# Causal masks of a fused attention and ELU-MLP kernel: products on VectorE against affine selects on GpSimd, in a newly planned order

## The chip, the cores and the metric

The kernel runs on one core of a Trainium2 chip. The metric is the device time of one execution in microseconds (us), given as the median of several runs; a profiled execution has a time of its own and a trace. The engines are TensorE (PE, with its weight loads as PEld), VectorE (DVE), ScalarE (ACT), GpSimd (POOL) and SyncE (SP). POOL and SP also issue most of the DMAs. Each engine works through its own instructions strictly in order.

## The reference, cut to what matters

The inputs are q, k and v with 8 batches, 8 heads, 576 positions and 64 columns per head, and 16 "beacon" keys and values per batch and head. The beacons stand ahead of the keys and are seen by every query; among the 576 keys, a query sees only those up to its own position. The result of the attention is laid out as 4608 tokens of 512 columns and goes through two matrix products with an ELU between them.

```python
scores = scale * np.matmul(q, k_all.transpose(0, 1, 3, 2))
causal[:, Nb:] = np.triu(np.ones((S, S), dtype=bool), k=1)
scores = np.where(causal, -1000000000.0, scores)
a = np.exp(scores - scores.max(-1, keepdims=True))
a /= a.sum(-1, keepdims=True) + 1e-09
x = np.matmul(a, v_all)          # then to (4608, 512)
h = x @ w_in
g = np.where(h > 0.0, h, np.exp(np.minimum(h, 0.0)) - 1.0)
out = g @ w_out
```

## The kernel before, in words

**The order.** All work is cut into some thirty kinds of steps, and the string at the end of the kernel (run, L793) lists 1430 of them in one hand-over order. A step is a word such as `x.3.4` or `m.3.0.1`; its fields are the batch or tile and the part of it. The list does not synchronize the engines with each other: it fixes the order in which each engine gets its own instructions, and waits between engines come from the data alone. So what a step's place decides is what stands ahead of it on its own engine.

**Attention.** A batch b has 13 chunks of scores (batch 0 has 16 smaller ones). `S.b.i` (L318) multiplies keys by queries on PE into PSUM, keys along the partitions; pairs of heads p = 0 to 3 follow each other along the columns, and parts that the mask would remove whole are not computed at all. `x.b.i` (L333) is the exponential on ACT, from PSUM into the tile et in SBUF, in 16-bit floats. What is left of the mask is a triangle of 128 columns in each block of keys; it is applied to et after the exponential by `m`.

**The masks.** For batches 1 to 7 there are four steps per batch, `m.b.d.g` (from L344): d is a half of the heads (two pairs, four heads), g = 0 takes the key blocks 0 and 1 in one product, of 128 partitions by 1024 elements, with the constant triangle triu; g = 1 takes blocks 2 and 3 in one such product and block 4 (80 partitions by 320 elements) in another. All are `tensor_tensor` products on DVE in L338. Batch 0 has 12 steps `m.0.p.g` by pairs, with one to three smaller products each.

**After the masks.** `D.b.d.n` (L396, DVE) adds key blocks into one tile ahead of the row sums; `L.b.d` (L376, L422, PE) forms the row sums and a first part of the output; `n.b.d` (L437, L440, ACT) inverts them; `W.b.d` (L376, PE) multiplies by v; `M.b.d.i` (L474, DVE) scales the result into xT, the MLP's input.

**The MLP.** Tile t has 512 tokens (tiles 0 and 1 have 256 each). `F.t.i` (L514, PE) is a piece of the first product, `e.t.i` (L524, ACT) its exponential. The other side of the ELU is either `u.t.i` (a rectifier, on ACT in L530, or with `.v` on DVE in L532) with `k.t.i` (L544, DVE), or `r.t.i` (L551, DVE) with `g.t.i` (L556, DVE). `Z.t.n` (L566, DVE) forms sums and differences of quarters for a Strassen-like second product, `Q.t.a.b` (L618, PE) is a run of its matmuls, and `J.t.n` drains PSUM (L628 on ACT, or with `.v` on DVE; L635 on DVE) and sends the result out by SP. For the last two tiles the first product is of this kind too (`P`, `K`, `E`, `U`, `V`, `X`, `H`).

**GpSimd.** It issues the loads: q and k of batches 0 to 2 (`lq`, L136), v (`lv`, L144 and L149), the weights (`wi`, L160; `wo`, L163), and for batches 3 to 7 copies of q and k within DRAM (`lk`, L769), which SP's transposing DMAs (`lt`, L776) bring into SBUF. It also makes the identity and triu (`ident`, `tri`; L236, L238) and fills the beacon keys and padding of batches 3 to 7 (`lp`, L785, L786). The drains of the transposed q and k of batches 0 to 2 are `ck` on ACT and `cq` on DVE (both L277). The eight DMA semaphores of POOL are used in turn, so its DMA waits for the landing of the eighth before it; what is behind that DMA on POOL waits too.

Of the kernel before, what the change touches and what calls it, by code (L numbers as in the profile page):

```python
# [17 lines left out]
def kernel(  # L18
# [787 lines left out]
    x.0.3.1 lv.0.2 m.0.1.0 m.0.2.0 m.0.0.0 L.0.A m.0.1.2 n.0.A m.0.0.2 T.1.0.0 wi.2 m.0.3.2
    cq.1.0.0 S.0.2.1 W.0.A.1 x.0.2.1 W.0.A.0 S.0.1.1 x.0.1.1 T.1.1.0 M.0.A.1 S.0.2.2 M.0.A.0
    x.0.2.2 F.0.5 cq.1.1.0 e.0.5 lv.0.3.4 m.0.2.2 wi.1 m.0.0.3 m.0.1.3 S.1.5 S.1.1 x.1.5 m.0.3.3
    F.0.4 x.1.1 lq.1.0.4.8 wi.0 m.0.2.3 L.0.B cb.1.1 e.0.4 W.0.B.1 n.0.B S.1.3 cb.1.3 u.0.4.v
    M.0.B.1 u.0.5.v F.0.2 x.1.3 e.0.2 r.0.2 S.1.4 x.1.4 S.1.0 x.1.0 F.0.3 T.1.3.0 ck.1.3.0  # L810
    W.0.B.0 g.0.2 wi.3 k.0.4 S.1.12 m.1.0.0 k.0.5 M.0.B.0 e.0.3 F.0.1 x.1.12 T.1.2.0 S.1.10
    r.0.3 g.0.3 F.1.0 cq.1.2.0 cb.1.2 e.0.1 u.0.1 x.1.10 k.0.1 F.1.1 e.1.0 S.1.8 lq.2.0.0.4
    u.1.1.v u.1.0 k.1.0 x.1.8 F.0.0 e.1.1 S.1.9 S.1.6 u.0.0.v lq.2.0.4.8 F.0.6 k.1.1 x.1.9
    lp.3.1 e.0.0 T.2.1.0 F.1.3 x.1.6 u.0.6.v e.0.6 cq.2.1.0 S.1.11 cb.2.0 lv.1.0.1 e.1.3 x.1.11
    S.1.7 k.0.0 F.0.7 S.1.2 u.1.3.v F.1.5 x.1.7 x.1.2 T.2.0.0 k.0.6 lv.1.2.3.4 u.0.7.v e.0.7
    m.1.1.1 T.2.2.0 ck.2.0.0 u.1.5.v ck.2.2.0 m.1.1.0 wo.1 e.1.5 m.1.0.1 F.1.6 wo.3 k.0.7 L.1.1
    L.1.0 wo.0 F.1.2 e.1.6 wo.2 k.1.5 lk.3.0 u.1.6.v lk.3.1 F.1.4 cb.2.1 cb.2.2 n.1.1 M.1.1.0
    W.1.0 k.1.6 n.1.0 M.1.0.0 u.1.2 W.1.1 lv.2.2.3.4 u.1.4 M.1.0.1 lk.4.0 e.1.2 lv.3.2.3.4 k.1.3
    S.2.4 e.1.4 x.2.4 F.1.7 M.1.1.1 k.1.4 u.1.7 e.1.7 F.2.13 T.2.3.0 S.2.8 u.2.13 k.1.7 F.2.12
    e.2.13 x.2.8 F.2.9 u.2.12 cq.2.3.0 S.2.3 e.2.12 k.2.13 S.2.1 e.2.9 wt.1.0 k.1.2 x.2.3 F.2.2  # L820
    e.2.2 lv.2.0.1 Z.1.3.B Q.1.0.7 x.2.1 Q.1.7.14 u.2.9.v S.2.2 S.2.0 u.2.2 k.2.12 F.2.6 k.2.9
    Q.1.14.21 x.2.0 x.2.2 F.2.15 cb.2.3 wt.1.1 e.2.6 wt.2.1 u.2.6 u.2.15 Q.1.21.28 e.2.15
    m.2.0.0 S.2.6 S.2.5 wt.2.0 F.2.4 J.1.0 x.2.5 F.2.10 Z.1.1.B Z.1.2.B S.2.11 x.2.6 Q.1.28.35
    lt.3.0 lp.3.0 lt.3.1 k.2.15 e.2.4 wt.3.1 u.2.4.v k.2.4 Q.1.35.42 x.2.11 S.2.7 x.2.7 k.2.2
    S.2.9 J.1.1 e.2.10 F.2.7 Q.1.42.49 u.2.7.v lk.4.1 Z.1.4.B u.2.10 Q.1.56.63 F.2.11 D.2.0.0
    x.2.9 S.2.10 S.2.12 wt.3.0 e.2.7 k.2.10 F.2.1 x.2.12 Q.1.49.56 J.1.2 Q.1.63.70 u.2.11 e.2.11
    wt.4.1 k.2.7 Q.1.70.77 k.2.6 F.2.3 S.3.0 m.2.0.1 x.2.10 u.2.1 e.2.1 D.2.0.1 J.1.3.v S.3.2
    D.2.0.2 D.2.0.3 x.3.0 F.2.14 e.2.3 x.3.2 Q.1.77.84 k.2.1 Q.1.84.91 r.2.3 k.2.11 L.2.0 n.2.0
    e.2.14 J.1.4 lk.5.1 W.2.0 wt.4.0 Q.1.91.98 M.2.0.0 M.2.0.1 H.1.2 S.3.4 u.2.14 F.2.5 m.2.1.0
    x.3.4 e.2.5 S.3.8 u.2.5 m.2.1.1 x.3.8 S.3.10 Q.1.98.105 lk.5.0 F.2.0 k.2.5 x.3.10 e.2.0  # L830
    lv.3.0.1 k.2.14 L.2.1 g.2.3 J.1.5 n.2.1 u.2.0.v W.2.1 F.2.8 M.2.1.0 M.2.1.1 u.2.8 F.3.6
    S.3.3 e.2.8 x.3.3 H.1.1 S.3.6 F.3.13 e.3.6 k.2.8 lt.4.0 x.3.6 lk.6.0 lp.4.1 Q.1.105.112
    k.2.0 Q.2.0.7 S.3.1 u.3.13.v Z.2.3.B S.3.12 Q.2.7.14 lp.4.0 u.3.6 F.3.4 e.3.13 J.1.6.v
    x.3.12 Q.2.14.21 lt.4.1 x.3.1 Z.2.1.B S.3.11 u.3.4 x.3.11 S.3.9 x.3.9 F.3.2 k.3.6 J.2.0.v
    Q.2.21.28 Z.2.2.B e.3.2 e.3.4 S.3.7 k.3.13 S.3.5 x.3.5 m.3.0.0 r.3.2 Q.2.28.35 F.3.8 g.3.2
    F.3.12 x.3.7 S.4.1 lt.5.0 S.4.0 Q.2.35.42 e.3.8 J.2.1 u.3.8 e.3.12 Q.2.42.49 m.3.0.1 r.3.12
    g.3.12 F.3.15 x.4.1 D.3.0.0 D.3.0.1 D.3.0.2 D.3.0.3 x.4.0 S.4.2 S.4.5 Q.2.49.56 J.2.2 x.4.2
    k.3.4 x.4.5 F.3.10 S.4.4 Z.2.4.B lt.5.1 e.3.15 x.4.4 S.4.3 u.3.10.v lp.5.1 m.3.1.0 x.4.3
    r.3.15 Q.2.56.63 Q.2.63.70 L.3.0 g.3.15 lk.6.1 e.3.10 k.3.10 n.3.0 W.3.0 lp.5.0 M.3.0.0
    M.3.0.1 F.3.7 u.3.7 e.3.7 F.3.3 S.4.7 S.4.11 F.3.9 lv.4 J.2.3.v u.3.3 x.4.11 k.3.7 D.3.1.0  # L840
    m.3.1.1 D.3.1.1 D.3.1.2 e.3.3 e.3.9 u.3.9 Q.2.70.77 k.3.3 k.3.8 Q.2.77.84 F.3.11 D.3.1.3
# [103 lines left out]
```

## Time and profile before

| what | value |
|---|---|
| median of 3 runs | 330.53 us (330.32 to 330.69) |
| the profiled execution, its own time | 329.86 us |
| its span, first to last instruction | 328.2 us |
| around the span | 1.66 us |
| granted TensorE clock | 1.0 in all of it |
| GpSimd: share of the span, instructions | 26%, 109 |

Busy time of an engine is the union of its instructions' spans. Matmuls overlap each other and their ends are modelled, so a PE that is busy throughout may still not be at its peak; the distance from one matmul's start to the next tells more. Idle time of an engine is put down to what ended it.

### The profile page before, as it was taken

To read this page: it belongs to the slowest core of one execution; us is meant where nothing else is said; L and a number is where in the kernel's file an instruction comes from. 1 tells how busy PE (TensorE), PEld (TensorE's weight loads), DVE (VectorE), ACT (ScalarE), POOL (GpSimd) and SP (SyncE) were. 2 spreads that over 40 slices of the span, in tenths; PEclk is the share of its full clock that TensorE was granted. 3 is DMA by queue.
4 is the path that set the end of the run, shared out by engine and by line. 5 is a ranking of instruction groups with operands and counts; after the bars stand their busy time and mean duration, and the time that the engine had idled before them with its cause. 6 is when DMAs were issued, how large, how long until landed. Compare 5 with 4: busy or idle time off the path is not lost.

```text
span 328.2 us, 8827 instructions
## 1 busy us (share of the span) xinstructions
PE 318.5 (97%) x3648; PEld 215.7 (66%) x3648; DVE 296.9 (90%) x527; ACT 276.4 (84%) x449; POOL 85.2 (26%) x109
## 2 busy tenths in 40 slices
PE   7879999999999999999999999999999999999995
PEld 4656766566555655566555665566665888888884
DVE  2677998999998999999989989999999999999992
ACT  2979999998889897999999888988699598889930
POOL 8973791742705626004010500000000000000000
PEclk9999999999999999999999999999999999999999
DMA  9999999999999999995922792010110021111113
GB/s 115 169 190 206 172 167 185 151 151 154 174 173 154 136 172 151 188 116 61 160 82 58 77 106 84 12 34 2 66 34 33 2 96 34 34 65 34 35 64 128
DMA packets 130520, 34.65 MB, mean 106 GB/s; under 512 B 112816, under 2 KB 130480, under 8 KB 130480
## 3 DMA queue, kind: packets, MB, share of 16 engines
q0 software_dynamic: 95840, 18.49, 69.1%
q1 hardware_dynamic: 33920, 15.34, 23.8%
q8 instruction: 28, 0.46, 0.6%
q10 hardware_dynamic: 720, 0.26, 0.3%
q14 instruction: 12, 0.10, 0.1%
HBM read 37.22 MB, written 15.34 MB: 160 GB/s over the span
## 4 chain that ended last, share of the span: by engine, by line
PE 72%; DMA 12%; ACT 7%; POOL 4%; DVE 3%; issue 2%; DVEq 0%; POOLq 0%
PE ops L618 27%; PE hps L514 22%; DMA v<-in_v_dram 10%; PE hps L706 8%; PE sc L318 5%; ACT et L333 5%; PE ut L376 5%; PE sx L618 2%; POOL scr L769 1%; POOL v L149 1%; DMA kst<-in_k_dram 1%; ACT e L524 1%; POOL w_out L163 1%; DVE qkp L396 1%; PE lt L422 1%
## 5 line engine op out<-in xcount | busy, mean ns | idle before, releaser
L333 ACT ACTIVATE et<-sc 128x1024 f16<-128x1024 f32 (+2 forms) x114 | 104.2, 968 | 8.1 <-PE sc L318 7.6
L514 PE MATMUL hps<-xT,w_in 128*128 128x512 f16 (+1 forms) x512 | 110.7, 353 | 0.3 <-DVE gt L556 0.3
L618 PEld LDWEIGHTS <-gt 128*128 128x128 f16 x864 | 83.0, 98 | 21.1 <-issue 2.9
L524 ACT ACTIVATE e<-hps 128x512 f32<-128x512 f32 x112 | 66.7, 615 | 9.0 <-PE hps L514 4.1
L514 PEld LDWEIGHTS <-w_in 128*128 128x128 f16 x512 | 46.8, 98 | 39.0 <-issue 5.5
L544 DVE SCALAR_TENSOR_TENSOR gt<-e,r 128x512 f16<-128x512 f32 x103 | 68.6, 683 | 2.2 <-ACT e L524 0.7
L618 PE MATMUL ops<-w_out,gt 128*128 128x256 f16 x416 | 54.7, 273 | 0.0
L618 PE MATMUL ops<-wt,gt 128*128 128x256 f16 x400 | 53.6, 273 | 0.0
L530 ACT ACTIVATE r<-hps 128x512 f16<-128x512 f32 x74 | 45.0, 616 | 4.5 <-PE hps L514 4.3
L149 POOL DMA_DIRECT2D v<-in_v_dram x40 | 36.4, 1016 | 3.5 <-DMA v<-in_v_dram 1.9
L566 DVE TENSOR_TENSOR gt<-gt 128x2048 f16<-128x2048 f16 (+1 forms) x30 | 33.1, 1110 | 0.1
L338 DVE TENSOR_TENSOR et<-et,triu 128x1024 f16<-128x1024 f16 (+4 forms) x66 | 26.6, 447 | 1.8 <-ACT et L333 1.7
L532 DVE TENSOR_SCALAR r<-hps 128x512 f16<-128x512 f32 x29 | 19.9, 685 | 4.0 <-ACT e L524 3.2
L376 PEld LDWEIGHTS <-v 128*32 128x32 f16 (+1 forms) x800 | 17.2, 96 | 9.4 <-issue 1.2
L745 DVE SCALAR_TENSOR_TENSOR gt<-e,r 128x512 f16<-128x512 f32 x32 | 21.5, 683 | 0.5 <-ACT kst L716 0.4
L376 PE MATMUL ut<-et,v 128*32 128x464 f16 (+3 forms) x560 | 21.1, 296 | 0.3 <-DMA v<-in_v_dram 0.3
L396 DVE TENSOR_TENSOR qkp<-qkp,et 128x1344 f16<-128x1344 f16 (+2 forms) x33 | 19.2, 583 | 0.4
L635 DVE TENSOR_TENSOR osb<-ops,sm 128x512 f32<-128x512 f32 x26 | 17.7, 682 | 1.3 <-PE ops L618 1.3
L716 ACT COPY kst<-hps 128x512 f32<-128x512 f32 x24 | 13.9, 589 | 4.8 <-PE hps L706 4.6
L474 DVE TENSOR_TENSOR xT<-ut,rl 128x672 f16<-128x672 f32 (+12 forms) x26 | 16.4, 669 | 0.7 <-PE ut L376 0.4
L618 PE MATMUL ops<-w_out,s 128*128 128x256 f16 x128 | 16.9, 273 | 0.0
L618 PEld LDWEIGHTS <-s 128*128 128x128 f16 x144 | 13.9, 98 | 2.5
(118 smaller groups left out, 415.7 us busy)
## 6 DMA issues: line engine op xcount, KB each, us to landing
out_dram<-osb SPq DMA_DIRECT2D x35, 256.0 KB, 2.2
v<-in_v_dram POOLq DMA_DIRECT2D x24, 128.0 KB, 11.8
scr<-in_q_dram POOLq DMA_DIRECT2D x5, 576.0 KB, 16.2
scr<-in_k_dram POOLq DMA_DIRECT2D x5, 576.0 KB, 18.1
w_in<-in_moe_w_in_dram POOLq DMA_DIRECT2D x8, 256.0 KB, 8.7
w_out<-in_moe_w_out_dram POOLq DMA_DIRECT2D x4, 512.0 KB, 10.5
qst<-in_q_dram POOLq DMA_DIRECT2D x4, 288.0 KB, 9.6
kst<-in_k_dram POOLq DMA_DIRECT2D x4, 288.0 KB, 10.0
```

What stands on the lines that cost most here:

```text
L149: nc.gpsimd.dma_start(out=vt[b][r0:r0 + n, j, :, :], in_=v[b, :, ilo[j]:ilo[j] + n, :].rearrange("h s d -> s h d"),)
L333: nc.scalar.activation(out=ets[b, d][:, :, a - EC2 * d:e - EC2 * d], in_=sc[b, g][:, :, a - c0:e - c0], func=AFT.Exp, bias=0.0, scale=SCALE)
L338: nc.vector.tensor_tensor(out=o, in0=o, in1=i, op=ALU.mult)
L376: nc.tensor.matmul(out=t[32 * i:32 * (i + 1), a - qa:e - qa], lhsT=ones[0:kc[j], :] if half is None else v16[0:kc[j], j, h, half:D:2], rhs ...
L396: nc.vector.tensor_tensor(out=o, in0=t[0:rows, :, a:e] if n == 0 else o, in1=t[0:rows, :, col:col + e - a], op=ALU.add)
L514: nc.tensor.matmul(out=h[:, n_, :], lhsT=w_in16[:, cc, P * fc:P * (fc + 1)], rhs=xt[k][:, cc, a - TT * k:e - TT * k], start=(cc == 0), sto ...
L524: nc.scalar.activation(out=eb[t, i], in_=flat(hp[t, i]), func=AFT.Exp, bias=0.0, scale=1.0)
L530: nc.scalar.activation(out=rb[t, i], in_=flat(hp[t, i]), func=AFT.Relu, bias=0.0, scale=1.0)
L544: nc.vector.scalar_tensor_tensor(out=half(t, i), in0=eb[t, i], scalar=1.0, in1=rb[t, i], op0=ALU.subtract, op1=ALU.min)
L566: (nc.vector if eng == "v" else nc.gpsimd).tensor_tensor(out=o_, in0=a_, in1=b_, op=op_)
L618: nc.tensor.matmul(out=half_of(xy[t, n_], qd), lhsT=lw[:, P * qd:P * (qd + 1)], rhs=wt_[:, c, :], start=(first and c == 0 and (qd == 0 or ...
L706: nc.tensor.matmul(out=hx[t, g, n_][:, c, :], lhsT=lw, rhs=rh, start=(first and c == 0 and k_ == 0), stop=(k_ == 1), skip_group_check=True)
```

## The change

A new function `cut` masks one key block by an affine select on GpSimd: it keeps an element where `base - partition + column >= 0` and writes 0.0 elsewhere, in place, for four heads at once (two in batch 0). The step `m` gets an engine letter. With `.p`, a mask of batches 1 to 7 is two selects for g = 0 (blocks 0 and 1) and three for g = 1 (blocks 2, 3 and 4) in place of one and two products.

```diff
+    def cut(o, base):
+        nc.gpsimd.affine_select(
+            out=o, in_=o, compare_op=ALU.is_ge, fill=0.0, base=base, channel_multiplier=-1,
+            pattern=[[0, o.shape[1]], [1, o.shape[2]]])
...
-    def m(b, p, g):
+    def m(b, p, g, eng="v"):
...
             t = et4(b, p)
+            if eng == "p":
+                for j in (0, 1) if g == 0 else (2, 3, 4):
+                    c, w = lays[b][j][3], min(P, lays[b][j][2] - lays[b][j][1])
+                    cut(t[0:kc[j], :, c:c + w], NB if j == 0 else 0)
+                return
...
-            mask(t[0:kc[j], :, col + a - qa:col + e - qa], triu[0:kc[j], 1:3, t0:t0 + e - a])
+            o = t[0:kc[j], :, col + a - qa:col + e - qa]
+            if eng == "p":
+                cut(o, t0)
+            else:
+                mask(o, triu[0:kc[j], 1:3, t0:t0 + e - a])
```

The list has 1430 steps before and after. Counted by their words, 28 masks carry the letter p: 24 of the 28 of batches 1 to 7 (all but m.1.1.0, m.5.0.1, m.5.1.1 and m.6.0.1) and 4 of the 12 of batch 0. Of the 24, 13 have g = 0 and 11 have g = 1. Besides, other choices of engine in the list differ:

| step | before | after |
|---|---|---|
| `u` on ACT / on DVE | 74 / 29 | 70 / 38 |
| pairs `r`, `g` | 9 | 4 |
| `k` | 103 | 108 |
| `ck` (ACT) / `cq` (DVE) | 5 / 11 | 3 / 13 |
| `J` with `.v` | 10 | 11 |

The order of POOL's own work, where the masks enter it:

```diff
-lq.1.0.0.4 lv.0.0.1 tri lv.0.2 wi.2 lv.0.3.4 wi.1 lq.1.0.4.8 wi.0 wi.3 lq.2.0.0.4 lq.2.0.4.8 lp.3.1
-lv.1.0.1 lv.1.2.3.4 wo.1 wo.3 wo.0 wo.2 lk.3.0 lk.3.1 lv.2.2.3.4 lk.4.0 lv.3.2.3.4 lv.2.0.1 lp.3.0
-lk.4.1 lk.5.1 lk.5.0 lv.3.0.1 lk.6.0 lp.4.1 lp.4.0 lp.5.1 lk.6.1 lp.5.0 lv.4 lk.7.0 lk.7.1 lv.5
-lp.6.0 lp.7.0 lp.6.1 lv.6 lp.7.1 lv.7
+lq.1.0.0.4 lv.0.2 tri m.0.1.0.p lv.0.0.1 wi.2 lv.0.3.4 wi.1 lq.1.0.4.8 m.0.2.3.p m.0.1.2.p wi.0
+m.0.3.2.p wi.3 lq.2.0.0.4 m.1.0.0.p lq.2.0.4.8 lv.1.2.3.4 lv.1.0.1 wo.3 lp.3.0 wo.0 m.1.1.1.p
+m.1.0.1.p wo.2 wo.1 lk.3.0 lk.3.1 lv.2.2.3.4 lv.2.0.1 lk.4.0 lk.4.1 m.2.0.0.p lk.5.0 m.2.0.1.p
+m.2.1.0.p m.2.1.1.p lv.3.0.1 lp.3.1 lv.3.2.3.4 lk.5.1 lk.6.0 lp.4.1 lp.4.0 lp.5.0 m.3.0.0.p
+m.3.1.0.p m.3.1.1.p m.3.0.1.p lk.6.1 lp.5.1 lk.7.0 lv.4 m.4.0.0.p lk.7.1 m.4.0.1.p lp.6.1 m.4.1.0.p
+m.4.1.1.p lp.6.0 m.5.0.0.p lv.5 m.5.1.0.p lp.7.1 m.6.0.0.p lv.6 lp.7.0 m.6.1.1.p m.6.1.0.p lv.7
+m.7.0.1.p m.7.0.0.p m.7.1.0.p m.7.1.1.p
```

Each engine's order differs in many places; PE gets the same matmuls. Around the three places where masks and their readers lie close together, the list after reads:

```text
F.0.7 S.1.2 x.1.7 k.0.0 e.1.3 k.0.6 u.0.7.v wo.0 x.1.2 e.0.7 T.2.0.0 cq.2.0.0 F.1.5 m.1.1.1.p m.1.1.0
k.1.3 e.1.5 k.0.7 T.2.2.0 F.1.6 ck.2.2.0 e.1.6 L.1.1 n.1.1 u.1.5.v m.1.0.1.p L.1.0 n.1.0 u.1.6.v F.1.4
...
lp.5.0 r.3.12 S.4.1 m.3.0.0.p x.3.7 S.4.0 D.3.0.0 m.3.1.0.p g.3.12 m.3.1.1.p Q.2.35.42 J.2.1 k.3.13 x.4.1
x.4.0 u.3.8.v F.3.10 e.3.10 S.4.2 S.4.5 x.4.5 u.3.10.v m.3.0.1.p D.3.0.1 D.3.0.2 Q.2.42.49 lk.6.1 J.2.2.v
...
S.7.12 x.7.12 F.7.8 e.7.8 k.6.2 Z.6.3.B k.6.7 Q.5.84.91 H.4.2 L.7.0 m.7.1.0.p W.7.0 e.6.15 u.7.8 J.5.4
Q.5.91.98 u.6.15.v D.7.1.0 F.7.7 n.7.0 M.7.0.0 u.7.7 k.6.15 m.7.1.1.p D.7.1.1 e.7.7 Q.5.98.105 Q.5.105.112 D.7.1.2
```

More of the change, by code (lines that the diff above doesn't have):

```diff
@@ L806 @@
[L806 to L841, printed above, removed]
@@ new lines @@
+    V.8.3.1 X.9.2 E.8.3.6 Q.7.77.84 J.7.4 U.8.3.6 Q.7.84.91 P.9.0.1 V.8.3.6 E.8.3.5 X.9.4
+    K.9.0.0 P.9.0.2 K.9.0.1 U.8.3.5 Q.7.91.98 J.7.5 K.9.0.2 U.9.0.1 P.9.0.3 K.9.0.3 P.9.0.4
+    V.8.3.5 E.9.0.1 K.9.0.4 Q.7.98.105 U.9.0.4 V.8.3.4 P.9.0.5 E.9.0.4 P.9.0.6 E.9.0.6
+    Q.7.105.112 K.9.0.5 U.9.0.6 Q.8.0.7 P.9.1.0 P.9.1.1 Z.8.3.B V.9.0.6 K.9.1.0 J.7.6 Q.8.7.14
+    P.9.1.2 Q.8.14.21 U.9.0.5 Z.8.1.B K.9.1.1 P.9.1.3 E.9.0.5 V.9.0.4 K.9.1.2 J.8.0 Z.8.2.B
+    U.9.1.1 Q.8.21.28 V.9.0.5 P.9.1.4 K.9.1.3 Q.8.28.35 P.9.1.5 K.9.1.4 E.9.1.1 P.9.1.6
@@ L916 @@
+    Q.8.98.105 K.9.3.5 E.9.3.5 E.9.3.4 V.9.3.1 U.9.3.5.v V.9.3.5 P.9.3.6 Q.8.105.112 E.9.3.6
+    U.9.3.4 Z.9.3.1 U.9.3.6 J.8.6 V.9.3.4 V.9.3.6 Z.9.1.1 Q.9.0.7 Q.9.7.14 Z.9.2.0 Q.9.14.21
+    Z.9.2.1 J.9.0 Q.9.21.28 Q.9.28.35 Q.9.35.42 J.9.1 Q.9.42.49 J.9.2.v Q.9.56.63 Q.9.63.70
+    Z.9.4.1 Z.9.4.0 Q.9.49.56 Q.9.70.77 J.9.3 Q.9.77.84 Q.9.84.91 J.8.5 J.9.4 Q.9.91.98
+    Q.9.98.104 J.9.5 Jh.9.0 Q.9.104.112 Jh.9.1
     """)
```

186 lines of the change are left out of this document (106 added, 80 removed).

## The prediction

> **What bounds the kernel now.** I read the page's part 1 first, then its chain by engine.
>
> ```profile
> span 328.2 us, 8827 instructions
> ...
> PE 318.5 (97%) x3648; PEld 215.7 (66%) x3648; DVE 296.9 (90%) x527; ACT 276.4 (84%) x449; POOL 85.2 (26%) x109
> ...
> PE 72%; DMA 12%; ACT 7%; POOL 4%; DVE 3%; issue 2%; DVEq 0%; POOLq 0%
> ```
>
> PE is busy for 97% and carries 72% of the chain. DVE, the engine that the change unloads, is at 90% but carries 3%. Busy shares are averages, so the table by stretches comes next; its columns are the busy times of PE, PEld, DVE, ACT and POOL with their instructions, the clock, the DMA share and GB/s.
>
> ```profile
> 25.00:50.00 25.00, 24.48 (x464) 17.90 (x463) 22.05 (x45) 24.69 (x35) 17.13 (x21) 1.00 1.39 182
> ```
> ```profile
> 50.00:225.00 175.00, 173.83 (x1893) 104.59 (x1891) 166.55 (x280) 157.90 (x249) 47.21 (x53) 1.00 1.28 120
> ```
>
> From 50 to 225 us, where nearly all masks lie, PE idles 175.00 - 173.83 = 1.17 us. Whether a busy PE is at its peak shows in the chain in order of time (start, us, what):
>
> ```profile
> 24.75 1.93 ACT et L333 x2
> ...
> 28.61 0.94 ACT et L333
> 30.99 1.03 ACT et L333
> 32.05 1.26 PE ub L376 x40
> ...
> 40.10 2.98 POOL w_out L163 x4
> 43.07 4.45 POOL scr L769 x2
> 48.13 18.65 DMA v<-in_v_dram
> 67.28 15.68 DMA v<-in_v_dram
> ...
> 195.48 0.86 PE hps L514 x4
> 196.34 1.53 PE ops L618 x14
> ```
>
> Four matmuls of 512 columns take 0.86 us and fourteen of 256 columns 1.53 us: 0.215 and 0.109 us each, the same time per column, and the second group starts where the first ends (195.48 + 0.86 = 196.34). That is a PE at its rate. Up to 32 us the chain is ACT's exponentials; the two loads of v, up to 83 us, run beside a PE that hardly waits. The longest waits of PE from 25 us on:
>
> ```profile
> PE sc L318 <- POOL qst L786: 0.3, 1, 0.3
> PE ut L376 <- DMA v<-in_v_dram: 0.3, 1, 0.3
> PE hps L514 <- DVE gt L556: 0.3, 1, 0.3
> ```
>
> So DVE is nearly full, yet what it does late costs PE almost nothing. Taking work off DVE cannot by itself bring more than these tenths.
>
> **The change, part by part.** What DVE loses and gets, by shape:
>
> ```profile
> L544 DVE SCALAR_TENSOR_TENSOR gt<-e,r 128x512 f16<-128x512 f32 x103 | 68.6, 683 | 2.2 <-ACT e L524 0.7 <-PE ops L618 0.7 <-ACT r L530 0.4
> ...
> L532 DVE TENSOR_SCALAR r<-hps 128x512 f16<-128x512 f32 x29 | 19.9, 685 | 4.0 <-ACT e L524 3.2 <-PE hps L514 0.3
> L338 DVE TENSOR_TENSOR et<-et,triu 128x1024 f16<-128x1024 f16 x28 | 18.9, 682 | 0.6 <-ACT et L333 0.5
> ...
> L556 DVE TENSOR_TENSOR gt<-hps,r 128x512 f16<-128x512 f32 x9 | 6.2, 691 | 0.3
> L628 DVE COPY sm<-ops 128x512 f32<-128x512 f32 x7 | 4.8, 681 | 0.0
> ...
> L551 DVE TENSOR_SCALAR r<-e 128x512 f16<-128x512 f32 x9 | 4.5, 497 | 1.5 <-ACT e L524 1.5
> L338 DVE TENSOR_TENSOR et<-et,triu 80x320 f16<-80x320 f16 x14 | 4.4, 315 | 0.0
> L277 DVE COPY qkp<-tp 128x1152 bf16<-128x1152 bf16 x3 | 4.1, 1358 | 2.1 <-PE tp L264 2.1
> ...
> L338 DVE TENSOR_TENSOR et<-et,triu 128x256 f16<-128x256 f16 x8 | 2.3, 282 | 0.0
> ```
>
> Removed: 13 masks with g = 0 at 0.682 = 8.9 us, 11 with g = 1 at 0.682 + 0.315 = 11.0 us, and four of batch 0, seven products of at most 0.282, some 1.8 us: 21.7 us. Added: nine rectifiers at 0.685 = 6.2, two drains `cq` at 1.358 = 2.7, one drain `J` at 0.681; five pairs of r and g (0.497 + 0.691) become five `k` (0.683): -2.5. DVE falls by 21.7 - 7.1 = 14.6 us to 282. ACT:
>
> ```profile
> L530 ACT ACTIVATE r<-hps 128x512 f16<-128x512 f32 x74 | 45.0, 616 | 4.5 <-PE hps L514 4.3
> ...
> L277 ACT COPY qkp<-tp 128x1152 bf16<-128x1152 bf16 x1 | 1.1, 1119 | 0.0
> ```
>
> Four rectifiers fewer (2.5 us), two `ck` fewer (2.2 us), one drain `J` fewer (0.6): -5.3 us. PE's matmuls are the same.
>
> On POOL, 13 x 2 + 11 x 3 = 59 selects come, and 7 small ones for batch 0. The trace has selects of other widths:
>
> ```profile
> L238 POOL TENSOR_SCALAR_AFFINE_SELECT triu<-triu 128x256 f16<-128x256 f16 x1 | 0.4, 402 | 0.0
> ...
> L238 POOL TENSOR_SCALAR_AFFINE_SELECT triu<-triu 128x128 f16<-128x128 f16 x1 | 0.3, 287 | 0.1
> ```
>
> A line through both (0.172 us and 0.898 ns for each element) gives 0.632 us for 512 elements and 0.460 for 320. A mask with g = 0 then takes 1.26 us on POOL and one with g = 1 takes 1.72, against 0.68 and 1.00 on DVE; all 24 take 35.4 us. POOL has the room: 47.21 of 175 us are busy. The Trainium skill (GPSIMD Engine Reference, Performance versus the Vector engine) measures about 1.8 cycles an element at best for a tight loop, which would make 512 elements 0.77 us (an estimate from that page) and the 24 masks some 43 us; no run here shows 512.
>
> The open price is what a select costs DVE while both work on SBUF. What the trace has, from the timelines of POOL and of DVE (start, us):
>
> ```profile
> 143.66 0.21 POOL L786 COPY qst<-bkT 128x32 bf16<-128x32 bf16 x1 [12.65 <-PE sc L318]
> ...
> 170.26 0.93 POOL L786 COPY kst<-bkT 128x32 bf16<-128x32 bf16 x1 [13.69 <-PE sc L318]
> ```
> ```profile
> 143.62 0.68 DVE L635 TENSOR_TENSOR osb<-ops,sm 128x512 f32<-128x512 f32 x1
> ```
> ```profile
> 169.90 1.22 DVE L566 TENSOR_TENSOR s<-gt 128x2048 f16<-128x2048 f16 x1
> ```
> ```profile
> 104.68 4.12 POOL L149 DMA_DIRECT2D v<-in_v_dram  x4
> ```
> ```profile
> 105.60 1.02 DVE L551 TENSOR_SCALAR r<-e 128x512 f16<-128x512 f32 x1 [1.20 <-ACT e L524]
> ```
>
> The same small copy takes 0.21 us beside L635, which has one input in PSUM, and 0.93 beside L566, whose inputs are both in SBUF: it ends at 171.19, 0.07 after DVE's instruction (169.90 + 1.22 = 171.12). So POOL waits for DVE. The other direction shows once: L551 beside POOL's DMA issues takes 1.02 us where its mean is 0.497. That a long select holds up DVE's two-input products is not shown. The bounds for a select are therefore nothing (it always waits for DVE) and its whole 0.46 to 0.63 us. The Trainium skill (SBUF — State Buffer, Who interferes with whom) says that the pair of ports which DVE's second SBUF input shares with GpSimd is an exclusive lock, held for a whole instruction; by that rule the upper bound is near, and the time that of the first rival.
>
> I take 0.25 us a select, under half of its length, because much of DVE's work (L532, L635, L556, the drains from PSUM) reads SBUF through one input at most. Between 50 and 225 us there are 51 selects (42 of 512, 9 of 320; 30.7 us). DVE there loses masks of 12 x 0.682 + 9 x 0.997 = 17.2 us and gets back 4.7 us of the 7.1 added (two `cq`, one rectifier and two r and g pairs of them belong before 50 us): 166.55 - 12.5 = 154.0. With 51 x 0.25 = 12.8 us it is at 166.8 of 175, as full as before, and PE went through that with 1.17 us idle. So this edit costs about nothing at that price; the cover is DVE's 21 us of spare time.
>
> Four terms then make the sum.
> - ACT's lead at the start. In 25 to 50 us ACT is the fullest (24.69 of 25.00) and the chain is on it. It loses two drains (2.2 us) and gets one rectifier more (0.6): 1.6 less. PE's idle time there is 25.00 - 24.48 = 0.52, though the gaps hidden in modelled spans may be more. Bounds 0 and 1.6, nearer to the idle row: -0.9.
> - The waits for v at 83 us and for POOL's L786, 0.3 each. In the new order the last part of v of batch 2 is issued ahead of both copies `lk.4`, and `lp.4` sooner after the load it follows: -0.5. Next late would be the second PE wait, 0.3.
> - Lateness of masks. Each select chain is longer than its product, and what reads the result sits close behind at three places: L.1.0 directly behind m.1.0.1.p, D.3.0.1 behind m.3.0.1.p, the fourth of four masks queued on POOL after lp.5.0 (6.0 us together), and D.7.1.1 behind m.7.1.1.p. A late D holds the `k`, `u` and `J` behind it on DVE, and these hold PSUM, so PE. Elsewhere L comes 8 to 28 us after the last needed scores in PE's order (counted with the rates above). From 0 to 3 us: +0.3, as the lengths alone still fit.
> - DMAs behind masks on POOL. m.1.0.1.p waits for x.1.2 and holds back wo.2, wo.1 and lk.3.0, which went out from 40.10 and, with `lk.3`, from 43.07 us. ACT's x.1.2 and 1.7 us of selects put them about 6 us later; the DMA engines have the loads of v and half of w_out before that, so I count 0. Without this cover the price is a gap in the DMA queue, up to 3 us (the half of 6 that half of w_out doesn't fill), paid by S.3.
>
> Sum: -0.9 - 0.5 + 0.3 + 0 = -1.1 us on the profiled execution's 329.86 us (its span of 328.2 and 1.66 around it): 328.8. The median shown, 330.53, is 0.67 above that execution, so the forecast for the median is **329.4 us**.
>
> **The rivals.** *Selects hold up DVE (slower).* Place: every `k`, `D` and `Z` that starts behind a running select, 50 to 225 us. For it speaks L551's doubled time, against it that the only case of two SBUF inputs shows POOL waiting. It decides from 21/51 = 0.41 us a select: above that DVE is fuller than its stretch. At 0.5 us, 25.5 us make DVE 179.5 of 175, so PE waits 4.5 us: 329.4 + 4.5 = 333.9; with the full length 30.7, it would be some 339.
> *PE's sum stands (no change).* The removed waits are replaced by others, since the matmuls are the same and PE idles 1.17 us in 175: 330.5, give or take 0.6. For it speaks the PE row; against it ACT's part of the chain before 32 us.
> *Masks too late on POOL (slower).* The queue of waits, issues and selects on one in-order engine runs behind, the third term at its upper end and a part of the fourth: from 329.4 + 2.7 = 332.1 to 335.1, say 333. For it: POOL stood 8.26 us at one DMA issue near 60 us.
>
> ```profile
> 59.63 2.20 POOL L769 DMA_DIRECT2D scr<-in_q_dram  x1 [8.26 <-issue]
> ```
>
> Against it: PE waited 0.3 us in all for POOL before. That the change does nothing of what it says is excluded by the list: 24 masks do leave DVE.
>
> **How the numbers follow.** Forecast 0.44, port rival 0.26, no change 0.18, late masks 0.12. A measurement of this kernel can tell about 0.2% (0.7 us). The no-change case is "same"; I leave "faster" the forecast's 0.44 and "slower" the other two, 0.38. The forecast's own range, from its terms' bounds, is 327.8 to 330.3. The range over the cases goes from 327.8 to 334.0, which takes in the port rival at 0.5 us a select and leaves out its upper end.
>
> **What would show it.** Right: DVE's `k` stays at 683 ns beside selects and DVE's busy time between 50 and 225 us at or under 167 us; selects of 512 elements at 0.63 us; no wait of PE for v at 83; ACT less full in 25 to 50 us. Wrong: `k`, `D` or `Z` stretched by tenths of a us where POOL runs a select; PE waiting for DVE's L396 or POOL's selects; L.1.0 waiting for POOL; the DMA queue running empty near 48 us.

## The result, and the profile after

The changed kernel takes 339.93 us in the median of 4 runs (338.73 to 341.40), the kernel before 330.42 (330.04 to 330.69, 4 runs): a ratio of 1.029, with an interval from 1.0245 to 1.0336. It is 9.5 us slower where 1.1 us faster was forecast, and above the range's upper end of 334.0. The profiled execution took 340.54 us. Lines behind `m` carry numbers that are 14 higher than before: `k` is L558, `u` with `.v` L546, `D` L410, `Z` L580, `L` L436, `Q` L632; the selects are L341.

From the page of the changed kernel: the span, the busy time of each engine, and the chain that ended last.

```profile
span 338.8 us, 8879 instructions
PE 322.3 (95%) x3648; PEld 217.0 (64%) x3648; DVE 301.5 (89%) x492; ACT 273.7 (81%) x442; POOL 138.1 (41%) x175
PE 58%; DVE 27%; ACT 9%; issue 5%; DVEq 0%; ACTq 0%
```

DVE's share of the chain was 3% and is 27%: PE now waits for DVE. The stretch from 50 to 225 us, and what PE waited for in all (total, times, longest):

```profile
50.00:225.00 175.00, 169.82 (x1849) 101.26 (x1845) 163.32 (x247) 152.34 (x235) 94.79 (x104) 0.99 1.25 120
```
```profile
PE lt L436 <- DVE qkp L410: 5.3, 4, 2.9
```

In the window PE does 4.0 us less than before (169.82 against 173.83), and yet DVE is less busy too, 163.32 us against 166.55. What stops PE is `L`, the row sums, waiting for `D`. The groups of DVE and POOL by shape (count, busy time, mean ns of one):

```profile
L558 DVE SCALAR_TENSOR_TENSOR gt<-e,r 128x512 f16<-128x512 f32 x108 | 76.3, 727 | 4.7 <-ACT e L538 2.4 <-ACT r L544 2.2
L580 DVE TENSOR_TENSOR gt<-gt 128x2048 f16<-128x2048 f16 x24 | 31.0, 1292 | 0.1
L546 DVE TENSOR_SCALAR r<-hps 128x512 f16<-128x512 f32 x38 | 25.7, 683 | 3.0 <-PE hps L528 1.6 <-ACT e L538 0.9
L410 DVE TENSOR_TENSOR qkp<-et 128x1856 f16<-128x1856 f16 x11 | 13.1, 1189 | 0.0
```
```profile
L341 POOL TENSOR_SCALAR_AFFINE_SELECT et<-et 128x512 f16<-128x512 f16 x48 | 41.6, 925 | 81.7 <-ACT et L333 52.3 <-issue 29.4
L341 POOL TENSOR_SCALAR_AFFINE_SELECT et<-et 80x320 f16<-80x320 f16 x11 | 11.3, 1024 | 1.5 <-ACT et L333 1.5
```

`k` was 683 ns and is 727 in the mean, `Z` (L580) 1217 and 1292, the first `D` 1115 and 1189; these have both inputs in SBUF. `u` on DVE (L546), which reads PSUM, was 685 and is 683. The selects of 512 elements take 0.63 us where DVE's instructions beside them have at most one input in SBUF (eleven cases), and 0.925 in the mean of all. So both sides wait. Adding up, for every DVE instruction, what it takes above the median of its shape before (differences over 0.03 us) gives a stretch of 15.9 us (before, by the same sum, 0.3): 0.27 us for each of the 59 selects. The waits of DVE show that the masks' readers hardly stand at the semaphore:

```profile
DVE qkp L410 <- POOL et L341: 0.5, 1, 0.5
```

The place of the largest single loss is the chain of waits between 117 and 131 us (start, us, what):

```profile
117.64 1.49 DVE xT L488 x3
119.12 1.13 DVE gt L580
120.25 0.34 DVE gt L558
120.59 1.21 issue
121.81 1.54 DVE qkp L410
123.35 1.04 DVE gt L558
124.39 0.60 DVE osb L649
124.99 1.02 DVE gt L558
126.01 1.22 DVE qkp L410
...
127.25 0.91 DVE qkp L410
...
128.18 0.64 DVE qkp L410
128.82 0.14 issue
128.96 0.38 PE lt L436 x4
```

Every `k` takes over 1 us instead of 0.68 (the first, from 120.17, 1.71 by the timeline, which the chain shows as 0.34 and 1.21 of issue), and the four `D` some 1.5, 1.2, 0.9 and 0.6 instead of 1.12, 0.85, 0.58 and 0.32, while POOL issues `lv.4` and runs m.4.0.0 and m.4.0.1. `L.3.1` starts at 128.96 after PE's longest wait, 2.86 us. Then a second price follows, the clock (a window of the same kernel; the column before the last two is the granted clock):

```profile
129.50:133.50 4.00, 4.00 (x19) 2.33 (x19) 3.44 (x6) 2.89 (x5) 0.21 (x1) 0.57 2.16 143
```

In the trace the clock stands at half from 129.88 us for 3.41 us, which is worth 1.7 us. The Trainium skill (TensorE: Matmul & The Clock Gate, What's actually happening) tells of a monitor that gates PE's clock by its recent activity; this row is in line with it. That the wait of 2.86 us brought the spell on is likely, but not shown. Of the runs told below, order_only and after_copy have such a spell beside waits of 2.05 and 2.47 us. But six others (before_nomask, after_free, after_fill, after_every2, after_pieces, after_lv) have one that begins between 22.9 and 24.1 us, behind idle times of PE of 0.8 to 1.7 us, and in five traces idle times of 1.0 to 1.3 us at that place bring none. It also comes and goes between executions of one kernel: run beside order_only, the kernel before took 329.75 to 330.04 us at a mean granted clock of 0.999 to 1.0, and 331.25 to 331.81 us at 0.993 to 0.995. A difference of up to 1.7 us can therefore be the clock's.

To place the rest, I add up the columns of all matmuls in their order, weighted by the share of the array that each uses, and compare when the sum of before's trace at a time t is reached in another trace (lag in us; a worked-out table, not a view):

```text
at t =               50     75    110    130    200    240    320
changed kernel      1.5    2.5    3.1    7.5    8.0   10.7   10.6
order_only          3.2    2.6    7.0    6.7   10.9   15.0   14.9
after_six           0.8    1.2    1.6    1.3    3.0    5.9    5.9
after_lv            2.2    2.3    2.7    3.8    4.6    7.4    7.2
after_nomask        0.7    0.1   -0.6   -0.9   -0.8   -0.8   -0.9
```

The changed kernel loses 1.5 us by 50 us, 4.4 between 110 and 130 (1.7 of them by the clock), and 2.7 between 200 and 240, where `L.6.1` and `L.7.1` wait 0.9 us each for `D` (PE's waits between 200 and 250 us):

```profile
PE lt L436 <- DVE qkp L410: 1.7, 2, 0.9
```

The other rows are experiments, told next; a spell of half clock is also in the rows of order_only (by 110 us) and after_lv (by 50 us).

### The profile page after: what moved, and what is told of

It is laid out like the page before. It is cut to its first block, busy times and chain, and to the rows that moved or that the text cites. A ratio compares the mean times of both kernels' runs of the same rounds, so it can differ in the third digit from the quotient of the medians.

```text
span 338.8 us, 8879 instructions
## 1 busy us (share of the span) xinstructions
PE 322.3 (95%) x3648; PEld 217.0 (64%) x3648; DVE 301.5 (89%) x492; ACT 273.7 (81%) x442; POOL 138.1 (41%) x175
## 4 chain that ended last, share of the span: by engine, by line
PE 58%; DVE 27%; ACT 9%; issue 5%; DVEq 0%; ACTq 0%
PE ops L632 21%; PE hps L528 14%; DVE gt L558 8%; PE hps L720 7%; ACT et L333 5%; DVE qkp L410 5%; PE sc L318 4%; PE ut L390 4%; DVE gt L580 3%; DVE r L546 2%; PE sx L632 2%; DVE xT L488 2%; ACT e L538 2%; PE lt L390 1%; DVE osb L649 1%
## 5 line engine op out<-in xcount | busy, mean ns | idle before, releaser
L632 PEld LDWEIGHTS <-gt 128*128 128x128 f16 x864 | 83.3, 98 | 23.7 <-issue 3.5
L341 POOL TENSOR_SCALAR_AFFINE_SELECT et<-et 128x512 f16<-128x512 f16 (+4 forms) x66 | 54.0, 883 | 83.2 <-ACT et L333 53.8
L558 DVE SCALAR_TENSOR_TENSOR gt<-e,r 128x512 f16<-128x512 f32 x108 | 76.3, 727 | 4.7 <-ACT e L538 2.4
L632 PE MATMUL ops<-w_out,gt 128*128 128x256 f16 x416 | 55.2, 276 | 0.0
L632 PE MATMUL ops<-wt,gt 128*128 128x256 f16 x400 | 53.4, 273 | 1.8 <-DVE gt L580 1.3
L544 ACT ACTIVATE r<-hps 128x512 f16<-128x512 f32 x70 | 41.9, 610 | 10.1 <-PE hps L528 6.8
L149 POOL DMA_DIRECT2D v<-in_v_dram x40 | 35.4, 1037 | 0.8 <-DMA w_out<-in_moe_w_out_dram 0.5
L580 DVE TENSOR_TENSOR gt<-gt 128x2048 f16<-128x2048 f16 (+1 forms) x30 | 34.8, 1170 | 0.1
L546 DVE TENSOR_SCALAR r<-hps 128x512 f16<-128x512 f32 x38 | 25.7, 683 | 3.0 <-PE hps L528 1.6
L410 DVE TENSOR_TENSOR qkp<-qkp,et 128x1344 f16<-128x1344 f16 (+2 forms) x33 | 22.2, 673 | 1.1 <-POOL et L341 0.5
L759 DVE SCALAR_TENSOR_TENSOR gt<-e,r 128x512 f16<-128x512 f32 x32 | 21.3, 682 | 0.2
L632 PE MATMUL ops<-w_out,s 128*128 128x256 f16 x128 | 17.3, 273 | 0.0
L632 PEld LDWEIGHTS <-s 128*128 128x128 f16 x144 | 13.8, 98 | 3.1 <-issue 0.4
```

The lines of the kernel that those rows point to most:

```text
L149: nc.gpsimd.dma_start(out=vt[b][r0:r0 + n, j, :, :], in_=v[b, :, ilo[j]:ilo[j] + n, :].rearrange("h s d -> s h d"),)
L341: nc.gpsimd.affine_select(out=o, in_=o, compare_op=ALU.is_ge, fill=0.0, base=base, channel_multiplier=-1, pattern=[[0, o.shape[1]], [1, o. ...
L410: nc.vector.tensor_tensor(out=o, in0=t[0:rows, :, a:e] if n == 0 else o, in1=t[0:rows, :, col:col + e - a], op=ALU.add)
L544: nc.scalar.activation(out=rb[t, i], in_=flat(hp[t, i]), func=AFT.Relu, bias=0.0, scale=1.0)
L546: nc.vector.tensor_scalar(out=rb[t, i], in0=flat(hp[t, i]), scalar1=0.0, scalar2=None, op0=ALU.max)
L558: nc.vector.scalar_tensor_tensor(out=half(t, i), in0=eb[t, i], scalar=1.0, in1=rb[t, i], op0=ALU.subtract, op1=ALU.min)
```

## The experiments

The theory after the result was the port: a select on POOL and a DVE instruction with two inputs in SBUF exclude each other. Its rivals were the order (the new list is bad whoever does the masks), lateness (readers wait for longer masks) and the queue (DMAs behind selects come late). Each ratio is to the kernel before, run beside it; intervals are 95%.

### The list alone, the selects alone, and selects that nobody needs

**order_only**: the changed list, all masks on DVE.

```diff
-m.4.0.0.p
+m.4.0.0        (and so for all 28)
```

> The changed kernel's list word for word, but all masks are products on DVE again. Before is 330.5 us, the changed kernel 339.9. Port theory (a select on POOL and a DVE instruction with two inputs in SBUF shut each other out, which lengthened DVE's instructions by 15.9 us in all in the trace of the changed kernel): DVE loses that stretch and gets 12 x 0.68 + 9 x 1.00 = 17.2 us of masks back between 50 and 225 us, so it is as full as before, its instructions have their old lengths again (k 0.68 us, Z 1.22), and the time falls to 330 to 333 us. Order theory (the new list itself is slower, selects or not): 336 to 340 us.

Measured: 343.99 us, ratio 1.039 (1.035 to 1.0432). The expectation of the port theory fails here, and that of the order theory is exceeded: with the masks back on DVE the list is slower than with the selects. The stretch is gone (0.9 us in all), as the port theory says, but what is left isn't harmless. The window from 50 to 225 us and PE's first waits of this kernel:

```profile
50.00:225.00 175.00, 167.17 (x1831) 100.09 (x1823) 160.35 (x268) 149.42 (x231) 47.38 (x52) 0.99 1.23 116
```
```profile
PE lt L436 <- DVE qkp L410: 4.0, 3, 1.5
PE hps L528 <- DVE r L546: 2.1, 3, 0.8
PE hps L528 <- DVE gt L570: 2.1, 1, 2.1
```

DVE is busy 160.35 us of 175, less than in the kernel before, which kept PE busy with 166.55; a window in which PE waits holds less work. Over the whole kernel this list gives DVE more to do (304.3 us busy against 296.9), and it puts readers close behind DVE's work, as if the masks' time on DVE were free. Which of the two makes it 3.9% slower wasn't taken apart. Either way DVE is idle 14.65 us of the window while PE waits for it.

**selects_only**: the list of before, the same 28 masks as selects.

```diff
-m.4.0.0
+m.4.0.0.p      (and so for all 28)
```

> The list of the kernel before word for word, but the same 28 masks are selects on POOL. Port theory: the stretch comes with the selects, some 59 x 0.27 = 16 us, against 21.7 us of masks that leave DVE; where several selects lie ahead of a D or k, PE waits: 334 to 341 us, with k and Z above their lengths of before by tenths of a us. Order theory: the list of before keeps its time, 330 to 331.5 us. Lateness theory (the mask's reader stands waiting at a semaphore for POOL, the port costs little): 333 to 340 us with DVE or PE waits of several us for the selects and unstretched DVE instructions.

Measured: 338.13 us, ratio 1.0204 (1.0164 to 1.0245); `k` has a mean of 743 ns, and the stretch is 15.7 us. DVE is busy 294.8 us in all, no more than the 296.9 of the kernel before, in the same list, and the kernel is 2.0% slower all the same. Lateness, which forecast a similar time, isn't the reason: DVE waits 0.5 us for POOL, as in the changed kernel.

```profile
PE 319.4 (95%) x3648; PEld 215.7 (64%) x3648; DVE 294.8 (88%) x485; ACT 276.8 (82%) x449; POOL 137.8 (41%) x175
...
L558 DVE SCALAR_TENSOR_TENSOR gt<-e,r 128x512 f16<-128x512 f32 x103 | 74.7, 743 | 4.9 <-ACT e L538 2.4 <-ACT r L544 1.5 <-PE ops L632 0.7
```

**before_extra**: the kernel before, with selects added whose result nobody reads.

```diff
 m.4.0.0
+y.4.0.0     # on POOL: affine_select(out=a tile of its own, in_=the masked block, 96 of 128 columns)
```

> The kernel before with all its masks on DVE, and behind 24 of them selects of the same blocks on POOL that nobody waits for: they read the masked exponentials (96 of 128 columns, so 384 elements and some 0.52 us each) and write to a tile of their own, 59 in all; an extra load, not part of the result. Port theory: no relief for DVE, and a stretch of 0.27 x 0.52/0.63 = 0.22 us a select, 59 x 0.22 = 13 us; DVE is at 166.6 of 175 us between 50 and 225, so it overflows by 2 to 5 us and PE waits in clumps besides: 333 to 341 us. Order theory and lateness theory: nobody waits for these selects, 330.5 to 331.5 us.

Measured: 348.99 us, ratio 1.0546 (1.0511 to 1.0582): above every expectation, and for another reason. The stretch is only 8.0 us. The selects wait on POOL for DVE's masks, and POOL's DMAs stand behind them (waits of POOL, then of PE):

```profile
POOL scrat L388 <- DVE et L338: 82.6, 12, 15.8
```
```profile
PE ops L643 <- DMA w_out<-in_moe_w_out_dram: 3.6, 2, 2.2
PE ut L401 <- DMA v<-in_v_dram: 3.1, 4, 1.5
PE lt L401 <- DMA v<-in_v_dram: 1.8, 1, 1.8
```

As a price of the port this run is no use. It shows what the queue costs in a list not made for it: PE waits 8.5 us for DMAs, for none of which it waits in the changed kernel.

**after_six**: the changed kernel, with the masks m.4.0.0, m.4.0.1 and the four of batch 7 on DVE.

> The changed kernel with six of its masks as products on DVE again, at the two places where PE fell behind in the trace: m.4.0.0 and m.4.0.1 (115 to 130 us, 4 us and a stretch of half clock lost) and the four masks of batch 7 (205 to 240 us, 2.7 us lost); 44 of 59 selects stay. Port theory with the clumps as the place of the loss: 332 to 335.5 us. If the loss is spread over all selects by DVE's fullness: 15 of 59 selects, so a quarter of the 9.4 us comes back, 337 to 338.5 us. Order theory: 338 to 341 us.

Measured: 336.57 us, ratio 1.0169 (1.0136 to 1.0202). Between the two forecasts, and the table tells why: the 4.4 us at 110 to 130 are gone (with the half clock), while between 200 and 240 us 2.9 are lost as before, though no mask of batch 7 is on POOL. `L.7.1` waits 1.55 us there, with its masks on DVE, where it waits 0.85 in the changed kernel; `L.6.1`, whose masks are on POOL in both, waits 1.11 and 0.89.

### What the list is worth when the masks cost nothing

**after_nomask** and **before_nomask**: the 28 words left out of each list.

> The changed kernel's list without the 28 masks that became selects: neither engine does them (their triangles stay unmasked). The list is then relieved on DVE as the change meant it, with nothing on POOL in exchange. If the loss is the price of the selects (port, lateness or queue): the list itself is as good as before or better, 328 to 331.5 us. Order theory (the list is worse even when the masks cost nothing): 335 to 340 us. Between, 331.5 to 335: both have a part, divided at this time.

> The list of before without the same 28 masks (left out, as in after_nomask). PE idled 1.2 us in 175 before, so the relief of DVE can bring little: 328.5 to 330.3 us by every theory. It is the measure for after_nomask: the difference of the two is the price of the list alone.

Measured: 328.89 us, ratio 0.9951 (0.9915 to 0.9987), and 330.24 us, ratio 0.9972 (0.9938 to 1.0006). The list is not bad: with the masks free, it is 0.5% faster than the kernel before. The list of before with the same masks left out is 0.3% faster, and the two intervals overlap, so that the new list as such is better isn't shown. Its windows show PE busy throughout.

```profile
25.00:50.00 25.00, 24.37 (x469) 17.83 (x464) 21.07 (x34) 23.43 (x35) 18.00 (x22) 1.00 1.44 194
```
```profile
50.00:225.00 175.00, 174.95 (x1906) 105.97 (x1904) 158.79 (x264) 156.39 (x244) 45.25 (x52) 1.00 1.25 118
```

Order theory falls with that, and the whole distance from 0.9951 to 1.0291, 3.4% or 11.2 us, is what the masks cost on POOL, with what the clock adds.

### Which part of a select costs

**after_short**: all waits stay, each select covers 8 of the columns of a head.

```diff
-cut(t[0:kc[j], :, c:c + w], NB if j == 0 else 0)
+cut(t[0:kc[j], :, c:c + 8], NB if j == 0 else 0)
...
-cut(o, t0)
+cut(o[:, :, 0:8], t0)
```

> The changed kernel, but every select covers only 8 columns of a head's 128 (32 elements, some 0.2 us by the line through the lengths, 16 in batch 0); the rest of the triangle stays unmasked. All waits of POOL for the exponentials, and of D and L for POOL, stay. Port theory (price by the length of a select): within 1.5 us of after_nomask. Queue and lateness theory (POOL waits for exponentials and holds back what follows, readers wait for the select): most of the loss stays, within 3 us of the changed kernel's 339.9. Order theory: as after_nomask, 335 or more.

Measured: 329.36 us, ratio 0.9975 (0.9943 to 1.0007), stretch 0.1 us. The waits of POOL for the exponentials, of `D` and `L` for POOL, and the place of the selects between the DMAs cost 0.24% or 0.8 us by the medians (0.9975 - 0.9951), which is within the two intervals.

**after_free**: full-length selects that write a tile which nobody reads; the 12 masks on DVE left out as well.

> The changed kernel's list with the 66 selects at full length, but they write to a tile that nobody reads, so that D and L never wait for them; the 12 products that had stayed on DVE are left out as well (so nothing is masked). Port theory: the stretch of DVE stays, 0.27 us a select, and most of the loss with it: 334 to 339 us, against after_nomask. Lateness theory (readers waiting for the selects are what costs): within 1 us of after_nomask.

Measured: 337.09 us, ratio 1.0177 (1.0128 to 1.0227), stretch 12.7 us. DVE doesn't wait for POOL at all, and 2.3% (1.0177 - 0.9951, 7.5 us) of the 3.4% are there all the same. Up to 1.7 us of them can be the clock: its four executions were at 0.993 to 0.995, and its trace has the spell at 24.10 us. The other 1.1%, 3.8 us, hold the 12 products and the readers' waits for selects of full length, and weren't taken apart.

**after_fill** and **after_copy**: a memset, or a copy onto itself, of the same block on POOL.

```diff
-nc.gpsimd.affine_select(out=o, in_=o, ...)
+nc.gpsimd.memset(o, 1.0)
```
```diff
-nc.gpsimd.affine_select(out=o, in_=o, ...)
+nc.gpsimd.tensor_copy(out=o, in_=o)
```

> The changed kernel with a memset of the same block to 1.0 in place of each select (so nothing is masked there): POOL writes the same elements and reads none. By the 0.494 us of the memset of 384 elements in before it takes some 0.64 us for 512. If any access of POOL to SBUF shuts out DVE's second input: as the changed kernel, 336 to 341 us, with k and Z stretched beside the memsets. If only reading does: as after_short, 329 to 331 us.

> The changed kernel with a plain copy of the same block onto itself on POOL in place of each select (so nothing is masked there): it reads and writes the same elements. The memset that only writes cost DVE nothing (329.0 us). If reading SBUF from POOL is what shuts DVE out, k and Z are stretched again and the time is 335 to 342 us. If it is the select as an instruction, 329 to 330.5 us and unstretched DVE instructions.

Measured: 329.01 us, ratio 0.9953 (0.9925 to 0.9982), and 337.45 us, ratio 1.0217 (1.0168 to 1.0265). First the rows of the fill, then those of the copy:

```profile
L341 POOL MEMSET et<- 128x512 f16 x48 | 25.8, 569 | 96.2 <-ACT et L333 65.1 <-issue 30.9
L556 DVE SCALAR_TENSOR_TENSOR gt<-e,r 128x512 f16<-128x512 f32 x108 | 71.6, 684 | 3.5 <-ACT r L542 1.7 <-ACT e L536 1.6
```
```profile
L341 POOL COPY et<-et 128x512 f16<-128x512 f16 x48 | 42.6, 944 | 81.1 <-ACT et L333 51.6 <-issue 29.5
L556 DVE SCALAR_TENSOR_TENSOR gt<-e,r 128x512 f16<-128x512 f32 x108 | 76.2, 725 | 4.7 <-ACT r L542 2.5 <-ACT e L536 2.1
```

A memset of 512 elements takes 569 ns on POOL, nearly as long as a select, in the same places, with the same data to wait for on both sides: `k` (L556 here) keeps its 684 ns, the whole stretch is 0.5 us, and the list reaches its full gain. A copy, which reads as well, brings back 725 ns and 14.0 us. So POOL's reading of SBUF is what shuts out DVE's second input, and not the select as such. The Trainium skill (SBUF — State Buffer, Who interferes with whom) says just that: two SBUF inputs on DVE contend with a GpSimd instruction that reads SBUF, and not with one that only writes it. These two runs agree.

### Length, number and place

**after_half** (64 of 128 columns in each select) and **after_every2** (29 of the 59 selects, at full length) read nearly the same number of elements: 48 x 256 + 11 x 160 = 14,048 and 24 x 512 + 5 x 320 = 13,888.

```diff
+y = o[:, :, 0:o.shape[2] // 2]       (after_half; the select then on y)
```
```diff
-for j in (0, 1) if g == 0 else (2, 3, 4):
+for j in (1,) if g == 0 else (2, 4) if p == 0 else (3,):       (after_every2)
```

> The changed kernel, each select over 64 of its 128 columns only (256 elements, 0.40 us alone; 40 of 80 columns in the last block); the other half of the triangle stays unmasked. Between the full selects (339.9 us) and those of 32 elements (329.4). Port theory, price in proportion to elements: half of the 10.5 us comes back, 333.5 to 336 us. If the price has a threshold (a select that fits into a gap of DVE costs nothing): nearer to the short ones, 329.5 to 333 us.

> The changed kernel with 29 of the 59 selects of batches 1 to 7, each at full length (24 of 512 elements, 5 of 320; the other blocks stay unmasked): as many elements in all as with all selects at half length, which gave 331.7 us. If the price goes by elements in all: 331 to 332.5 us. If it goes by the number of full-length selects (half of the 10.5 us between full and short ones): 333 to 335.5 us, so that length itself is what costs.

Measured: 331.69 us, ratio 1.0028 (1.0005 to 1.0052), and 334.15 us, ratio 1.0103 (1.0063 to 1.0144). DVE's stretch is nearly the same, 6.1 and 6.5 us. In proportion to the elements it is not: the changed kernel reads twice as many and has 15.9. The time of after_half lies in the range of the threshold, that of after_every2 in the range of the price by full-length selects: the same stretch in few large pieces costs 0.75% or 2.5 us more. But most of this can be the clock. All ten executions of after_half were at 0.998 or more, three of the four of after_every2 at 0.993 to 0.995; the fourth, at full clock, took 332.61 us, 0.9 more than after_half. PE's wait for `D`, of after_half (line 411 there) and of after_every2:

```profile
PE lt L437 <- DVE qkp L411: 1.2, 2, 0.9
```
```profile
PE lt L436 <- DVE qkp L410: 2.5, 3, 1.3
```

**after_pieces**: the same elements as in the changed kernel, in pieces of 32 columns.

```diff
+for c in range(0, o.shape[2], 32):
+    y = o[:, :, c:min(c + 32, o.shape[2])]
...
```

> The changed kernel, each select cut into pieces of 32 columns for the four heads (128 elements, 0.287 us alone, four to a block of 128): the same elements are masked, the result is the reference's, POOL's instructions for it are four times as many and nearly twice as long together (some 1.15 us a block in place of 0.63). If a select shuts the port for the whole of its length: more of the loss, 341 to 347 us. If it shuts it for its elements only (0.898 ns each, 0.11 us a piece, 0.46 us a block), and DVE's next instruction gets its turn between pieces: the loss shrinks, as short ones find gaps in which DVE uses no second input, 332 to 337 us. Lateness theory: readers wait twice as long, 341 us or more.

Measured: 344.17 us, ratio 1.0405 (1.035 to 1.0459). The time lies in the range of the first theory, but its reason doesn't show: DVE's stretch is nearly halved (8.3 us), as the second theory has it. POOL pays for it: a piece takes 0.795 us in the mean where it alone takes 0.287, as if each waited for DVE anew, and now it is lateness that costs (waits of DVE, then of PE):

```profile
DVE qkp L412 <- POOL et L343: 6.4, 8, 2.2
```
```profile
PE sc L318 <- POOL kst L802: 1.4, 1, 1.4
```

**after_lv**: one word moved, in the place of the largest loss.

```diff
-F.3.14 lv.4 M.3.1.1 u.3.5 S.4.9 M.3.1.0 S.5.0 k.3.0 m.4.0.0.p k.3.5
+F.3.14 M.3.1.1 u.3.5 S.4.9 M.3.1.0 S.5.0 k.3.0 m.4.0.0.p lv.4 k.3.5
```

> The changed kernel with the step lv.4 (six DMA issues, 4.5 us on POOL) moved from ahead of the mask m.4.0.0 to behind it; nothing else. In the trace of the changed kernel a k at 120.17 us took 1.71 us while POOL was still issuing lv.4, ahead of the select. If a select that stands queued behind DMA issues shuts the port before it runs: the k and D beside lv.4 have their lengths of before again, D.3.1.3 comes 1 us or more earlier, PE's wait of 2.9 us at 129 us shrinks, 335 to 339 us. If the issues themselves stretch DVE, or if it was the selects' own time: the instructions beside lv.4 stay stretched, 339 to 341.5 us.

Measured: 336.98 us, ratio 1.0186 (1.0154 to 1.0218), 3 us less than the changed kernel. At like clocks (0.993 to 0.995) it is 337.25 and 337.74 us against 339.32 and 340.54. POOL and DVE in this run, from the timelines:

```profile
118.08 3.28 POOL L341 TENSOR_SCALAR_AFFINE_SELECT et<-et 128x512 f16<-128x512 f16 x2
120.30 1.53 POOL L144 DMA_DIRECT2D v<-in_beacon_v_dram  x1
120.82 5.22 POOL L149 DMA_DIRECT2D v<-in_v_dram  x5
125.00 3.27 POOL L783 DMA_DIRECT2D scr<-in_k_dram  x1
126.70 3.70 POOL L341 TENSOR_SCALAR_AFFINE_SELECT et<-et 128x512 f16<-128x512 f16 x3
```
```profile
122.28 0.68 DVE L558 SCALAR_TENSOR_TENSOR gt<-e,r 128x512 f16<-128x512 f32 x1
123.48 0.68 DVE L558 SCALAR_TENSOR_TENSOR gt<-e,r 128x512 f16<-128x512 f32 x1
124.08 1.28 DVE L410 TENSOR_TENSOR qkp<-qkp,et 128x1344 f16<-128x1344 f16 x1
125.39 0.90 DVE L410 TENSOR_TENSOR qkp<-qkp,et 128x832 f16<-128x832 f16 x1
```

Beside the issues of `lv.4`, with a DMA issue behind them in the queue, the two `k` have their 0.68 us. The two `D` that follow, beside the last issues of `lv.4` and that of `lk.7.1` (L783), take 1.28 and 0.90 instead of 0.85 and 0.58, and `lk.7.1` has m.4.0.1's selects directly behind it. The selects' recorded start, 126.70, is later than the end of both `D`. It isn't the issues alone: in the traces of the kernel before and of order_only, 186 DVE instructions with both inputs in SBUF lie beside nothing on POOL but DMA issues, and none is stretched by over 0.06 us. So a select that stands next in the queue seems to shut DVE out while POOL still issues the DMA ahead of it. POOL's spans are rough, so this is a reading of starts and not more; that the move itself gains 0.9% is measured.

No run is faster than the kernel before and masks everything. With the masks free this list gains 0.5%, so there was little for a better split to win, and none was tried.

## Why the prediction was wrong, step by step

**The step that failed** is "So this edit costs about nothing at that price; the cover is DVE's 21 us of spare time." The price in it was nearly right: 0.25 us a select was taken, 0.27 is measured. It was a choice between bounds of 0 and 0.63 us, so that it came so near is partly luck.

The cover was not there. To begin with, it was smaller than worked out. Without a stretch DVE was to be at 154.0 us in the window; after_nomask, with the relief and no masks on POOL, has 158.79. The sum took whole lengths off, but DVE's instructions overlap by some 0.08 us: in after_lv a `k` of 0.68 us starts at 123.48 and the next instruction at 124.08. That leaves 16.2 us of spare time and not 21. Still, 51 selects at 0.27 us are 13.8 us and would have fitted. So the step fails in its idea: idle time in one place doesn't cover a stretch in another. In the changed kernel DVE is idle 11.7 us of the window; but from 119 to 129 us it works without a break, every `k` and `D` in that stretch is lengthened, and `L` waits 2.86 us for the last `D`. selects_only shows it in the unchanged list: DVE is busy no longer than before, 294.8 us against 296.9, and the kernel is 2.0% slower. The sign that DVE stays at or under 167 us in the window came true (163.32) in a forecast that was wrong: a PE that waits brings less work into the window.

**The rival's threshold** fell with it. Selects that hold up DVE were to decide from 0.41 us each; in after_free, where they stretch DVE by 12.7 us or 0.22 us each, they cost 5.8 to 7.5 us against after_nomask. The mechanism was named, with a chance of 0.26, and its sign, PE waiting for `D` (L396 before), came; its size was derived from fullness, like the cover. Nor is the upper bound near, a select's whole length: of 0.63 us DVE loses 0.27 in the mean, and the select itself takes 0.29 longer.

**ACT's lead at the start (-0.9)** didn't come. ACT has 1.26 us less to do between 25 and 50 us in after_nomask (23.43 against 24.69), where 1.6 were counted, but PE is at 24.37 against 24.48, and the list is 0.7 us behind at 50 us. What the 0.5% of after_nomask consists of lies later.

**The waits for v and for POOL's copy (-0.5)** went, as said: neither is in the list of PE's waits after, and after_nomask goes from 0.7 us behind at 50 us to 0.6 ahead at 110.

**Lateness (+0.3)** had the right size for what waits at the semaphore: DVE waited 0.5 us for POOL in all, at 113.56 us, at `D.3.0.2`, just behind one of the three places named. What PE waits for is a `D` that was stretched, and the longest such wait, at `L.3.1`, is at none of them. **DMAs behind masks (0)**: right here, PE waits for none. before_extra shows the price where the list isn't made for it.

**The lengths of the selects** were right where DVE has at most one input in SBUF beside them (0.629 to 0.638 us against 0.632), and for the shortest of 320 elements (0.469 against 0.460); the other estimate, 0.77, was too long, and its sum over the 24 masks is 42 us, not 43. In the mean they take 0.925 and 1.024 us. **The lost clock** after a long wait of PE was in no step.

## What to carry to other kernels

Here, work moved to GpSimd wasn't free for VectorE as soon as it read SBUF: look for the VectorE instructions with two SBUF inputs beside it, price the stretch on both engines, and ask whether a form that only writes will do. An engine's idle share is no cover: look for what follows directly on the instructions that will be stretched, and who waits for that. And a list planned for a relief has to get it: the same list was 0.5% faster, 2.9% slower or 3.9% slower than before, depending on what the masks cost and where.
